# Moving one input load from SyncE's DMA queue to ScalarE's in a fused attention and feed-forward kernel

## The chip, the cores and the metric

The kernel runs on one NeuronCore of a Trainium2 chip. The metric is the device time of one execution in microseconds (us). "Span" is the length of the profiled execution; it is about 2 us shorter than the device time of the same run (323.9 against 325.91 in the profiled run of before).

A "granted clock" is TensorE's clock as a share of full speed. Each run lists its mean over the span. Of the twelve profiles with a windows view by the microsecond, the seven with a mean of 0.997 to 1.0 show 1.00 in every microsecond from 8 to 16 us, and the five with 0.990 to 0.994 show 0.50 there, for 3.4 us in the change, sync_last and v_first and for 6.8 to 6.9 us in cold_before and v_small (summed from the windows). Runs without a profile are sorted below by the same mean (under 0.9965 or not); where their low stretch lay is inferred. The clock record of a trace begins with the first rise of the clock (at 5.11 us in before). Before that the windows view prints 1.00, which is not a measurement: in before the weight loads of the warm-up matmuls come 0.43 us apart until then, and 12 in 2.47 us afterwards.

## The reference, cut to what matters

Linear attention with position weights, then a gated feed-forward layer. Inputs are float32, q, k and v of shape 8 x 8 x 576 x 64 (batch, heads, positions, head size), gate and value weights of 512 x 1536, output weights of 1536 x 512.

```python
r = np.maximum(x, 0.0)                      # for q and for k
phi = concatenate([r * cos_w, r * sin_w])   # cos and sin of the position
kv  = einsum('bhsf,bhsd->bhfd', k_p, v);  z = k_p.sum(axis=2)
x   = (q_p @ kv) / (q_p @ z + 1e-6)
g, val = x @ w_gate, x @ w_val
out = (gelu(g) * val) @ w_out
```

## The kernel before

TensorE is the busy engine for nearly the whole run (98% of the span). Only the first batch has nothing to hide behind: its q, k and v must arrive, be scaled by cosines (VectorE) and sines (ScalarE), and be transposed and multiplied, before TensorE has its long matmuls. The program order on each engine is fixed by hand. The parts that matter:

```python
def load(eng, name, b, m0, m1, j0=0, j1=R):      # R = 9 column groups of 64
    ...
    eng.dma_start(out=staged[name, b][:, m0:m1, j0 * D:j1 * D],
                  in_=rows(srcs[name], b)[:, m0:m1, j0 * D:j1 * D])

load(nc.sync, "k", 0, 0, 2)            # 576 KB, pieces of 2304 B
load(nc.sync, "k", 0, 2, 4)            # 576 KB
load(nc.sync, "q", 0, 0, NP, 0, JA)    # 512 KB, pieces of 1024 B (JA = 4)
load(nc.sync, "v", 0, 0, 2)            # 576 KB, pieces of 2304 B
load(nc.sync, "v", 0, 2, 4)            # 576 KB
load(nc.sync, "q", 0, 0, NP, JA, R)    # 640 KB, pieces of 1280 B
# ... ScalarE: a table load, sin_t, cos_t, a table load, a warm-up Gelu
...
# VectorE and ScalarE, in this order: k's cosines and sines, then
prep("q", 0, 0, range(JA))             # VectorE: q's cosines (L162)
cast_v(0, 0, 2, dve_copy)              # VectorE: v's first half to bf16 (L179)
nc.gpsimd.tensor_copy(gate, staged["v", 0][:, 0, 0:1])  # holds the weight loads back (L458)
load_w(0, 2)                           # GpSimd's queue: gate and value weights
...
dummies(22)                            # TensorE: warm-up matmuls on zeros (L140)
sines(0, 1, 2, 3)                      # ScalarE: q's sines (L160)
turn_j(0, 0, 2, (0, 1), 0, act_copy)   # TensorE: transposes of q (L204), copied out
cast_v(0, 2, 4, dve_copy)              # VectorE: v's second half
turn_j(0, 2, 4, (0, 1), 1, dve_copy)
kv_pairs(0, 0, 2, (6, 7))              # TensorE: k-v products (L218)
turn_j(0, 0, 2, (2, 3), 2, act_copy)
turn_j(0, 2, 4, (2, 3), 3, dve_copy)
...
kv_pairs(0, 2, 4, (4, 5))
...
nm_pair(0, 0, (6, 4))                  # TensorE: q times kv, two tiles (L307)
... # then the first block's gate and value products by tile (L372), and from L400 on the long ones
```

## Time and profile before

| | before |
|---|---|
| median of the first three runs | 326.79 us (326.55 to 327.45) |
| span of the profile | 323.9 us |
| TensorE busy | 98% of the span |
| bytes of the first batch's six loads | 3.54 MB |

The page gives the span, and the busy time and share of TensorE (PE), its weight loads (PEld), VectorE (DVE), ScalarE (ACT) and GpSimd (POOL). Its part on the chain that ended last follows:

```profile
PE 316.8 (98%) x2451; PEld 164.5 (51%) x2451; DVE 170.3 (53%) x407; ACT 159.3 (49%) x336; POOL 26.0 (8%) x43
PE 93%; DMA 2%; DVE 2%; SPq 1%; issue 0%; DVEq 0%
```

The chain of waits in order of time (start, duration, what) shows what the 2% of DMA are: the landing of v's second half, at 10.74 us, and then its cast.

```profile
2.82 7.92 DMA vf<-in_v_dram
10.74 0.02 issue
10.76 0.86 DVE vx L179
```

The DMA issues of the first 14 us give size and time from issue to landing. SyncE issued q's first part at 1.76, so it landed at 1.76 + 6.1 = 7.9.

```profile
vf<-in_v_dram SPq DMA_DIRECT2D x2, 576.0 KB, 7.5
qf<-in_q_dram SPq DMA_DIRECT2D x1, 512.0 KB, 6.1
```

The windows view gives, for each microsecond: its length, busy time (and instructions) of PE, PEld, DVE, ACT, POOL, then the granted clock, the DMA engines' share, and GB/s. The DMA engines are full (a share of 1.06 from 7 to 8 us and 1.46 from 13 to 14).

```profile
7.00:8.00 1.00, 1.00 (x6) 0.35 (x4) 1.00 (x2) 1.00 (x5) 0.90 (x1) 1.00 1.06 417
13.00:14.00 1.00, 0.95 (x20) 0.65 (x17) 0.93 (x5) 1.00 (x4) 0.41 (x1) 1.00 1.46 202
```

The timeline (start, duration, engine, line, operation, output<-input, count, and the idle time before it with what ended it) gives the opening's order:

```profile
1.52 6.67 PE L140 MATMUL ps<-dummy 128*128 128x512 bf16 x22 [1.52 <-POOL dummy L113]
8.09 1.13 DVE L162 TENSOR_SCALAR qp<-qf,cos_t 128x256 bf16<-128x256 f32 x4
8.52 1.69 ACT L160 ACTIVATE qp<-qf,sin_t 128x256 bf16<-128x256 f32 x4
9.06 0.23 PE L204 MATMUL ps<-ident,qp 128*128 128x128 bf16 x1 [0.87 <-ACT qp L160]
9.37 0.77 DVE L179 CAST vx<-vf 128x1152 bf16<-128x1152 f32 x1 [0.15 <-DMA vf<-in_v_dram]
9.39 0.77 POOL L458 COPY gate<-vf 128x1 f32<-128x1 f32 x1 [1.50 <-DMA vf<-in_v_dram]
12.59 0.76 PE L307 MATMUL ps<-kv_sb,qT 128*128 128x65 bf16 x16
16.48 0.61 PE L372 MATMUL ps<-xT,wg_sb 128*128 128x128 bf16 x8
21.11 1.03 PE L400 MATMUL ps<-xT,wg_sb 128*128 128x512 bf16 x4
```

Each input lands just before the engine that needs it is free: q just before 8.09, v's first half 0.15 us late for VectorE.

### The profile page before, as it was taken

To read this page: it belongs to the slowest core of one execution; us is meant where nothing else is said; L and a number is where in the kernel's file an instruction comes from. 1 tells how busy PE (TensorE), PEld (TensorE's weight loads), DVE (VectorE), ACT (ScalarE), POOL (GpSimd) and SP (SyncE) were. 2 spreads that over 40 slices of the span, in tenths; PEclk is the share of its full clock that TensorE was granted. 3 is DMA by queue.
4 is the path that set the end of the run, shared out by engine and by line. 5 is a ranking of instruction groups with operands and counts; after the bars stand their busy time and mean duration, and the time that the engine had idled before them with its cause. 6 is when DMAs were issued, how large, how long until landed. Compare 5 with 4: busy or idle time off the path is not lost.

```text
span 323.9 us, 6340 instructions
## 1 busy us (share of the span) xinstructions
PE 316.8 (98%) x2451; PEld 164.5 (51%) x2451; DVE 170.3 (53%) x407; ACT 159.3 (49%) x336; POOL 26.0 (8%) x43
## 2 busy tenths in 40 slices
PE   8899999999999999999999999999999999999995
PEld 3574556555754564545544554445544444444443
DVE  5854677759665952793586348544532222222211
ACT  7864858946466832673457336633222332222220
POOL 6684410000000000000000000000000000000000
PEclk9999999999999999999999999999999999999999
DMA  7999999842999689938957990543431111111124
GB/s 274 249 186 273 297 352 366 230 111 51 323 216 354 166 147 383 201 83 251 330 96 157 383 232 1 137 102 78 85 73 33 34 32 32 35 32 32 34 65 98
DMA packets 69102, 53.57 MB, mean 165 GB/s; under 512 B 45392, under 2 KB 54352, under 8 KB 69072
## 3 DMA queue, kind: packets, MB, share of 16 engines
q1 hardware_dynamic: 59264, 41.23, 48.1%
q0 software_dynamic: 9648, 11.80, 15.7%
q8 instruction: 19, 0.31, 0.4%
q10 hardware_dynamic: 160, 0.13, 0.1%
q14 instruction: 11, 0.09, 0.1%
HBM read 37.75 MB, written 9.44 MB: 146 GB/s over the span
## 4 chain that ended last, share of the span: by engine, by line
PE 93%; DMA 2%; DVE 2%; SPq 1%; issue 0%; DVEq 0%
PE ps L400 57%; PE ps L430 28%; PE ps L282 3%; PE ps L241 3%; DMA vf<-in_v_dram 2%; PE ps L204 1%; PE ps L372 1%; PE ps L697 1%; SPq L80 1%; PE ps L357 0%; DVE qp L162 0%; DVE x_sb L322 0%; DVE vx L179 0%; DVE x_sb L295 0%; DVE qT L486 0%
## 5 line engine op out<-in xcount | busy, mean ns | idle before, releaser
L409 DVE TENSOR_TENSOR hT<-gel,ps 128x512 bf16<-128x512 f32 (+1 forms) x114 | 74.1, 650 | 128.9 <-PE ps L400 126.0
L408 ACT ACTIVATE gel<-ps 128x512 f32<-128x512 f32 (+1 forms) x114 | 64.8, 569 | 109.7 <-PE ps L400 108.0
L400 PE MATMUL ps<-xT,wv_sb 128*128 128x512 bf16 (+1 forms) x456 | 110.2, 364 | 0.0
L400 PE MATMUL ps<-xT,wg_sb 128*128 128x512 bf16 (+1 forms) x456 | 110.2, 364 | 0.0
L430 PE MATMUL ps<-wo_sb,hT 128*128 128x512 bf16 x420 | 105.8, 379 | 0.0
L400 PEld LDWEIGHTS <-wv_sb 128*128 128x128 bf16 x456 | 44.6, 98 | 47.0
L400 PEld LDWEIGHTS <-wg_sb 128*128 128x128 bf16 x456 | 44.0, 98 | 46.1
L430 PEld LDWEIGHTS <-hT 128*128 128x128 bf16 x420 | 38.3, 98 | 39.4
L439 ACT COPY o_sb<-ps 128x512 f32<-128x512 f32 x34 | 19.9, 587 | 29.9 <-PE ps L430 27.6
L160 ACT ACTIVATE qp<-qf,sin_t 128x256 bf16<-128x256 f32 x72 | 32.0, 501 | 0.4 <-DMA qf<-in_q_dram 0.4
L160 ACT ACTIVATE kp<-kf,sin_t 128x256 bf16<-128x256 f32 (+1 forms) x73 | 29.9, 479 | 0.9 <-DMA kf<-in_k_dram 0.9
L295 DVE TENSOR_TENSOR x_sb<-ps,rec 128x512 bf16<-128x512 f32 x38 | 26.3, 691 | 1.3
L162 DVE TENSOR_SCALAR qp<-qf,cos_t 128x256 bf16<-128x256 f32 x71 | 21.8, 353 | 2.3 <-DMA qf<-in_q_dram 2.3
L282 PEld LDWEIGHTS <-qT 128*128 128x128 bf16 x304 | 14.6, 98 | 7.9 <-ACT qT L486 0.3
L162 DVE TENSOR_SCALAR kp<-kf,cos_t 128x256 bf16<-128x256 f32 x63 | 18.3, 349 | 0.0
L282 PE MATMUL ps<-kv_sb,qT 128*128 128x65 bf16 x304 | 16.0, 194 | 0.0
L179 DVE CAST vx<-vf 128x1152 bf16<-128x1152 f32 (+1 forms) x15 | 12.0, 804 | 0.8 <-DMA vf<-in_v_dram 0.8
L250 ACT CAST kv_sb<-ps 128x260 bf16<-128x260 f32 x14 | 4.6, 383 | 12.9 <-PE ps L241 12.9
L241 PEld LDWEIGHTS <-kp 64*128 64x128 bf16 x504 | 8.5, 95 | 3.0 <-issue 3.0
L140 PE MATMUL ps<-dummy 128*128 128x512 bf16 x27 | 8.4, 457 | 1.5 <-POOL dummy L113 1.5
L241 PE MATMUL ps<-vx,kp 64*128 64x65 bf16 x504 | 9.3, 191 | 0.0
L294 DVE RECIPROCAL rec<-den 128x8 f32<-128x8 f32 x38 | 7.7, 203 | 1.3
(60 smaller groups left out, 100.6 us busy)
## 6 DMA issues: line engine op xcount, KB each, us to landing
out_dram<-o_sb SPq DMA_DIRECT2D x70, 128.0 KB, 2.6
kf<-in_k_dram SPq DMA_DIRECT2D x12, 576.0 KB, 6.2
vf<-in_v_dram SPq DMA_DIRECT2D x12, 576.0 KB, 8.3
qf<-in_q_dram SPq DMA_DIRECT2D x10, 576.0 KB, 5.0
qf<-in_q_dram POOLq DMA_DIRECT2D x4, 576.0 KB, 12.2
kf<-in_k_dram POOLq DMA_DIRECT2D x4, 576.0 KB, 12.5
vf<-in_v_dram POOLq DMA_DIRECT2D x4, 576.0 KB, 12.8
wg_sb<-in_moe_w_gate_dram POOLq DMA_DIRECT2D x6, 256.0 KB, 6.4
```

Of the source, the lines that this page charges most:

```text
L140: nc.tensor.matmul(bank(to), lhsT=dummy[:, 0:128], rhs=dummy, start=True, stop=True)
L160: nc.scalar.activation(o, i, AF.Relu, scale=tab[:, j:j + 1])
L162: (eng or nc.vector).tensor_scalar(o, i, 0.0, tab[:, j:j + 1], op0=ALU.max, op1=ALU.mult)
L179: copy(vx_tiles[b % 2][:, m0:m1, j0:j1, 0:D], staged["v", b][:, m0:m1, j0 * D:j1 * D].rearrange("p m (j d) -> p m j d", d=D),)
L241: nc.tensor.matmul(bank(6 + i)[:, m * (D + 1):(m + 1) * (D + 1)], lhsT=kp[rr, m, j, :], rhs=vx[rr, m, j, :], start=(j == 0), stop=(j == R ...
L282: nc.tensor.matmul(bank(b0 + h // 4)[:, (h % 4) * (D + 1):(h % 4 + 1) * (D + 1)], lhsT=q_cols(b, t, h), rhs=kv_sb[b][:, h // 2, h % 2, :], ...
L295: nc.vector.tensor_tensor(x, nm[:, :, :, 0:D], rec[:, :, :, None].to_broadcast([128, 2, 4, D]), op=ALU.mult,)
L400: nc.tensor.matmul(bank(b0 + g)[:, 0:w], lhsT=wt[:, ct, js], rhs=xt[:, ct, c0:c0 + w], start=(ct == 0), stop=(ct == CT - 1),)
L408: nc.scalar.activation(gel[:, 0:w], bank(b0)[:, 0:w], AF.Gelu)
L409: nc.vector.tensor_mul(hT[n][:, jt, c0:c0 + w], gel[:, 0:w], bank(b0 + 1)[:, 0:w])
L430: nc.tensor.matmul(bank(to), lhsT=hT[n][:, jt, tt * 128:(tt + 1) * 128], rhs=wo_sb[:, jt, :], start=(jt == 0), stop=(jt == JT - 1),)
L439: copy(o_sb, bank(to))
```

## The change

The intent: two queues side by side, so that v need not queue behind q, and SyncE has one issue less.

```diff
     load(nc.sync, "k", 0, 0, 2)
     load(nc.sync, "k", 0, 2, 4)
-    load(nc.sync, "q", 0, 0, NP, 0, JA)
     load(nc.sync, "v", 0, 0, 2)
@@
     nc.scalar.activation(warm, half_pi, AF.Gelu)
+    load(nc.scalar, "q", 0, 0, NP, 0, JA)
```

## The prediction

> **What bounds the kernel now.** The page of the run before gives PE 98% of a 323.9 us span, and the chain of waits is 93% PE. From 19.1 us on TensorE hardly waits, so the change can only act in the opening. There the chain reads: SyncE's five issues (0.7 to 2.8 us), "DMA vf<-in_v_dram" for 7.92 us until v's second half lands at 10.74, VectorE's cast of it, qT copies, kv_sb, q's cosines, den/rec/x_sb, and TensorE from 16.1 us. What delays this chain delays everything after, nearly one for one.
>
> **What the opening waits for.** The windows view shows DMA saturated: share about 1.0 and 330 to 417 GB/s in every microsecond from 3 to 11. The six loads are 3.54 MB, which is what had moved by 12 us. So the order of bytes matters, not the time of issue: an issue costs 0.44 to 0.53 us on SyncE, while 576 KB take about 1.5 us. Landings, from issue and time to landing: k 4.5 and 5.9, q's first part 7.9, v 9.4 and 10.7, q's rest 12.4. Each comes just before its use: ScalarE's k sines end at 8.5 and its q sines run 8.52 to 10.2; VectorE's q cosines start at 8.09.
>
> **What the change does.** It takes one 0.47 us issue off SyncE (v is issued 0.5 us sooner, worth nothing behind a full queue) and puts one of about 0.54 us (ScalarE's two issues at the trace's end) on ScalarE after the warm-up Gelu, which ends at 4.0. ScalarE waits for k until 4.52 anyway. [...] So 512 KB of q will interleave with k or v instead of standing between them.
>
> When it is issued is my largest doubt: between 1 and 4.1 us. Near 4, q shares with v: k is untouched, q's packets (1024 B) alternate with v's (2304 B), and q lands between 8 and 10.7 us. Earlier (ScalarE's sequencer ahead of its table load), q slows k: k's second half lands 1 to 1.7 us later, q at 7.5 to 9.3. In both, v's second half stays near 10.7, since the same bytes precede it, and q's rest near 12.4. VectorE and ScalarE run in order and are nearly full from 4.5 to 12 us, so ScalarE's q sines move by 1 to 2 us, and VectorE's v casts, which stand behind the q cosines, by 0.3 to 1.9 us; its 0.6 us wait before the second cast absorbs part. Net: +0.5 to +1.9 us; I take +1.0. A gain would need v to land clearly sooner, which the bytes forbid.
>
> **Prediction.** 327.8 us, 8 times in 10 between 326.4 and 329.3. Faster by over 2%: 1%; within 2%: 97%; slower by over 2%: 2%.
>
> **What would show it right.** q's first part landing after 7.9 or k's second half after 5.9; v's second half still at 10.5 to 10.9; ScalarE's first q sine after 8.5; the second v cast after 10.76; the first full-width gate matmul (21.1 us) later by as much as the span. After that the timelines should be alike.
>
> **What would make it wrong.** The queues may share by bytes, so that q lands at 8.0 and nothing moves (0 to +0.2 us). ScalarE's queue may get more than its share. TensorE's gap after the warm-up matmuls (8.2 to 9.1 us) may grow to 3 us and cool its clock (about +1 us). v's first half landing sooner would release the weight loads against q's rest. None of these reaches 2% (6.5 us).

The sum: it came to +0.5 to +1.9 us, of which +1.0 was taken, on the 326.8 us of before. The "about +1 us" for a cooled clock stands outside the sum; it was the author's estimate.

## The result, and the profile after

| | before | after |
|---|---|---|
| median of six runs | 326.67 us (325.52 to 327.49) | 329.54 us (329.27 to 329.91) |
| span of the profile | 323.9 us | 327.3 us |
| mean granted clock | 0.998 | 0.992 |

The ratio is 1.0088, with a 95% interval of 1.0066 to 1.0111: slower by some 0.9%, well inside the 2%. A ratio here is the mean time of one kernel's runs over that of the other's of the same rounds, so it is not quite the ratio of the medians. The difference of the medians is 2.87 us.

The chain of waits in order of time now begins with q:

```profile
2.10 8.72 DMA qf<-in_q_dram
```

The DMA issues of the first 14 us: q takes 8.7 us instead of 6.1, and lands at 10.8.

```profile
vf<-in_v_dram SPq DMA_DIRECT2D x2, 576.0 KB, 7.2
qf<-in_q_dram ACTq DMA_DIRECT2D x1, 512.0 KB, 8.7
```

The timeline, the same operations as before:

```profile
1.52 6.53 PE L140 MATMUL ps<-dummy 128*128 128x512 bf16 x22 [1.52 <-POOL dummy L112]
2.10 0.51 ACTq L80 DMA_DIRECT2D qf<-in_q_dram  x1
8.14 0.18 POOL L458 COPY gate<-vf 128x1 f32<-128x1 f32 x1 [0.19 <-DMA vf<-in_v_dram]
10.84 1.70 ACT L160 ACTIVATE qp<-qf,sin_t 128x256 bf16<-128x256 f32 x4 [2.21 <-DMA qf<-in_q_dram]
10.85 1.27 DVE L162 TENSOR_SCALAR qp<-qf,cos_t 128x256 bf16<-128x256 f32 x4 [2.63 <-DMA qf<-in_q_dram]
11.41 0.23 PE L204 MATMUL ps<-ident,qp 128*128 128x128 bf16 x1 [3.36 <-ACT qp L160]
12.03 1.42 DVE L179 CAST vx<-vf 128x1152 bf16<-128x1152 f32 x2
15.86 0.77 PE L307 MATMUL ps<-kv_sb,qT 128*128 128x65 bf16 x16
19.84 0.61 PE L372 MATMUL ps<-xT,wg_sb 128*128 128x128 bf16 x8
24.48 1.03 PE L400 MATMUL ps<-xT,wg_sb 128*128 128x512 bf16 x3
```

Four things are to be seen.

1. The issue is at 2.10, as the first sine activation starts (2.09), long before the warm-up Gelu that stands ahead of it in the program (3.80). The trace shows that the issue waited neither for the second table load (2.51) nor for the Gelu, and not why.
2. v's first half is there by 8.14, but its cast runs at 12.03. VectorE has q's cosines ahead of it in program order, and q is not there.
3. The lag grows. The first transpose is 2.35 us late (11.41 against 9.06), the two-tile products 3.27 us (15.86 against 12.59), the first long matmul 3.37 us (24.48 against 21.11), the span 3.4 us.
4. TensorE now idles 3.36 us ahead of the first transpose.

The growth of the third goes with the fourth: without that gap, in warm_after below, the loss is 1.86 us. In the windows view the clock is at half soon after the first transpose (0.82 in the microsecond from 11 to 12, 0.98 in 15 to 16):

```profile
9.00:10.00 1.00, 0.00 (x0) 0.00 (x0) 0.00 (x0) 0.00 (x0) 1.00 (x3) 1.00 1.07 390
12.00:13.00 1.00, 0.90 (x14) 0.64 (x14) 1.00 (x3) 1.00 (x3) 0.00 (x0) 0.50 1.41 190
13.00:14.00 1.00, 1.00 (x37) 0.91 (x34) 0.78 (x2) 0.02 (x1) 0.54 (x2) 0.50 1.44 194
```

The clock record has one stretch of 3.412 us at 0.5 there, from 11.64 to 15.05. It begins 0.23 us after the gap of 3.36 us ends. In other profiles single gaps of 3.04 us (v_small), 3.14 (sync_last) and 3.91 (cold_before) between the warm-up and the first transposes came with a half clock too, and the longest waits before the first transposes of 0.87 (before), 1.37 (warm31), 1.69 (before18) and 1.96 us (early_issue) did not. Length alone does not sort them: in v_first, below, gaps of 1.18 and 1.93 us with 0.75 us of matmuls between them came with a half clock. What decides within this range is not shown.

Why q came so late is in the DMA queues' own packets (count, MB, share of the engines' time), q1 being SyncE's queue and q10 ScalarE's. From 4 to 5 us, and from 7 to 8 us:

```profile
q1 hardware_dynamic: 179, 0.41, 104.0%
...
q1 hardware_dynamic: 124, 0.26, 67.7%
q10 hardware_dynamic: 122, 0.12, 36.2%
```

Up to 5 us ScalarE's queue moved nothing, though q was issued at 2.10. Its first packet in the trace's DMA records starts at 5.61, after k's 512 packets (the 512th packet of 2304 B starts at 5.26). From 7 us on the two queues move packets in nearly equal number: 124 against 122, then 118 against 118 and 165 against 162 in the next two microseconds. A packet of q is 1024 B and one of v is 2304 B, so q gets a third of the bytes (0.12 of 0.39 MB from 7 to 8 us) and its 512 packets last nearly as long as v's 512: v's last packet starts at 9.8 and q's at 10.4, where before q's started at 7.53. The starts in the DMA records go with the counts: from 4 to 5 us the distances between packets of q1 pile up at 89 ns and its multiples, and from 7 to 8.6 us those within either queue pile up at 132 ns and its multiples. A packet of q1 takes 93 ns there and one of q10 46 (medians). I read this as one packet of each in turn; the records do not name the engine of a packet, so the turns themselves are not seen.

### The profile page after: what moved, and what is told of

Its sections match the earlier page's. It is cut to its first block, busy times and chain, and to the rows that moved or that the text cites. A ratio compares the mean times of both kernels' runs of the same rounds, so it can differ in the third digit from the quotient of the medians. Undisturbed runs are those within 1.5% of the kernel's fastest.

```text
span 327.3 us, 6303 instructions
## 1 busy us (share of the span) xinstructions
PE 315.3 (96%) x2414; PEld 165.3 (51%) x2451; DVE 170.6 (52%) x407; ACT 159.3 (49%) x336; POOL 25.3 (8%) x43
## 4 chain that ended last, share of the span: by engine, by line
PE 93%; DMA 3%; DVE 1%; issue 1%; ACT 0%; POOL 0%; DVEq 0%; POOLq 0%
PE ps L400 56%; PE ps L430 27%; PE ps L282 3%; PE ps L241 3%; DMA qf<-in_q_dram 3%; PE ps L204 1%; PE ps L372 1%; PE ps L697 1%; PE ps L357 1%; PE ps L218 1%; DVE qp L162 0%; ACT qp L160 0%; DVE x_sb L295 0%; DVE vx L179 0%; PE ps L140 0%
## 5 line engine op out<-in xcount | busy, mean ns | idle before, releaser
L430 PE MATMUL ps<-wo_sb,hT 128*128 128x512 bf16 x401 | 103.1, 379 | 1.4 <-issue 0.8
L204 PE MATMUL ps<-ident,qp 128*128 128x128 bf16 x72 | 6.8, 239 | 3.8 <-ACT qp L160 3.5
```

The source lines that it names most:

```text
L204: nc.tensor.transpose(out=dst[:, n * 128:(n + 1) * 128], in_=phi["q", b][:, m, j, :], identity=ident,)
L430: nc.tensor.matmul(bank(to), lhsT=hT[n][:, jt, tt * 128:(tt + 1) * 128], rhs=wo_sb[:, jt, :], start=(jt == 0), stop=(jt == JT - 1),)
```

## The experiments

My theory after the result: the queue does not matter, the order in which the bytes land does. q's last byte now comes behind most of v. This costs some 2 us by itself, and the idle gap it makes costs about 1 us more through the clock. The rivals: ScalarE's issue or its queue is slow; the clock is harmless; what costs is that the programs wait for q ahead of v. The medians of before on the same chip were 326.82 us for the first four experiments, 327.18 for the next two, 326.75 for the four after them and 326.85 for the last two.

| run | median, us | ratio to before (95% interval) | runs with a mean clock under 0.9965 |
|---|---|---|---|
| the change | 329.54 | 1.0088 (1.0066 to 1.0111) | 6 of 6 |
| sync_last | 329.41 | 1.0075 (1.0051 to 1.0099) | 3 of 4 |
| warm_after | 328.56 | 1.0057 (1.0040 to 1.0074) | 0 of 4 |
| cold_before | 327.48 | 1.0016 (0.9991 to 1.0041) | 4 of 4 |
| v_first | 329.49 | 1.0081 (1.0056 to 1.0105) | 4 of 4 |
| early_issue | 327.06 | 1.0021 (0.9989 to 1.0053) | 1 of 4 |
| v_small | 329.92 | 1.0072 (1.0023 to 1.0120) | 3 of 4 |
| warm31 | 329.06 | 1.0084 (1.0061 to 1.0108) | 2 of 6 |
| v_first_warm | 328.25 | 1.0046 (1.0029 to 1.0062) | 1 of 6 |
| before_again | 327.17 | none (one run) | 0 of 1 |
| before18 | 326.34 | 0.9993 (0.9975 to 1.0011) | 0 of 6 |
| gate_on_q | 326.77 | 1.0005 (0.9979 to 1.0032) | 3 of 6 |
| gate_on_q18 | 326.24 | 0.9991 (0.9968 to 1.0015) | 1 of 6 |

All gave correct results.

### The order alone, without ScalarE's queue (sync_last)

```diff
-    load(nc.sync, "q", 0, 0, NP, 0, JA)
     load(nc.sync, "v", 0, 0, 2)
     load(nc.sync, "v", 0, 2, 4)
+    load(nc.sync, "q", 0, 0, NP, 0, JA)
     load(nc.sync, "q", 0, 0, NP, JA, R)
```

> All six loads stay on SyncE, in the order k, k, v, v, q's first part, q's rest: ScalarE issues nothing. Theory (what costs is that q's last byte now arrives behind v's; the queue that carries it does not matter): q's first part lands near 10.6 us, v near 8.0 and 9.3, the first transposes start near 11.3, the clock drops as in the changed kernel, and the time is that of the changed kernel, before + 2.5 to 3.5 us. Rival (ScalarE's own issue, or a slow start of its queue, costs the time): time of before, within 0.7 us.

The timeline of this kernel, then its windows (columns as before):

```profile
10.47 1.71 ACT L160 ACTIVATE qp<-qf,sin_t 128x256 bf16<-128x256 f32 x4 [2.05 <-DMA qf<-in_q_dram]
```

```profile
13.00:14.00 1.00, 1.00 (x35) 0.91 (x30) 0.62 (x2) 0.00 (x0) 0.12 (x2) 0.50 1.40 189
```

With everything on SyncE and only q's place moved behind v, q's work starts at 10.47, the clock drops, and the time is, within the intervals, that of the change (1.0075 against 1.0088). ScalarE's queue is cleared: the change is, in effect, a reordering of the loads.

### The clock alone (warm_after, warm31, cold_before)

```diff
-    dummies(22)
+    dummies(37)      # warm_after, on the changed kernel
+    dummies(31)      # warm31, on the changed kernel
+    dummies(8)       # cold_before, on the kernel before
```

> The changed kernel with 37 warm-up matmuls instead of 22, so that TensorE is busy until q is there. Theory (about 2.4 us of the loss is q's lateness, about 0.9 us is TensorE's clock at 0.5 between 11.8 and 15 us): no drop of the clock, first transposes still near 11.4, the two-tile attention products near 15.0 instead of 15.86, time before + 1.8 to 2.6 us, about 0.9 below the changed kernel. Rival (the clock is harmless because the vector engines bound the opening): time unchanged against the changed kernel, before + 2.7 to 3.4 us.

> The kernel before with 8 warm-up matmuls instead of 22: TensorE idles from about 4.9 to 9.1 us, all loads as they were. Theory: the idle gap alone drops the clock to 0.5 for about 3 us from the first transposes on and costs 0.6 to 1.1 us. Rival (the clock is harmless): within 0.3 us of before.

> The changed kernel with 31 warm-up matmuls. With 37 they overshot: in that profile the clock rose only at 7.4 us, they ended at 12.5 and held up transposes whose q was ready at 11.7. With 31 they should end between 9.8 and 11.4 wherever the clock rises. Theory (the clock costs about 1 us of the loss, the rest is q's lateness): no drop of the clock in any run, time before + 1.5 to 2.2 us. Rival (the clock's part is all of it, and q's lateness is hidden): before + 0 to 0.7 us.

In warm_after no run had a low stretch, and the loss fell from 2.87 to 1.86 us (0.57% of 326.7). The windows and the timeline show how: TensorE is busy while it waits (1.00 in every microsecond from 8 to 12), the clock stays at 1.00, and the two-tile products come at 15.40 instead of 15.86.

```profile
9.00:10.00 1.00, 1.00 (x7) 0.44 (x5) 0.00 (x0) 0.00 (x0) 1.00 (x3) 1.00 1.05 389
13.00:14.00 1.00, 0.75 (x37) 0.70 (x38) 1.00 (x3) 0.33 (x1) 0.00 (x0) 1.00 1.43 191
```

```profile
15.40 0.77 PE L307 MATMUL ps<-kv_sb,qT 128*128 128x65 bf16 x16
```

Useless matmuls made the kernel faster by 0.9 us (its four runs took 328.44 to 328.93, the change's six 329.27 to 329.91; the means are 328.62 and 329.54). The two did not run in the same rounds, and the intervals of their ratios overlap. I thought 37 overshot (the first transposes came at 12.33, not near 11.4), and tried 31. This was a miss as a tuning: two of its six runs still met a low stretch. But it gives a difference within one kernel: its four warm runs have a mean of 328.83, its two others of 330.44, 1.6 us more. early_issue below has the same split (three runs with a mean of 327.03, one of 328.63); in sync_last it is 1.2 us and in v_first_warm 0.7. So a low stretch goes with about 0.7 to 1.6 us here. That the clock alone makes this difference within a kernel is not shown: in the runs that were not profiled q may also have landed later.

cold_before was to measure that on the kernel before. It lost 0.16%, about 0.5 us, and its interval (0.9991 to 1.0041) includes no loss at all as well as the 0.6 to 1.1 us that I expected. That is inconclusive. Its windows show the clock at 0.5 from about 8.8 to 15.7 us, twice as long as in the change, and its opening did lag: the two-tile products came at 14.12, against 12.59 and 12.94 in the two profiles of before.

```profile
14.12 1.08 PE L307 MATMUL ps<-kv_sb,qT 128*128 128x65 bf16 x16
```

Before's own scatter, told of below, may hide a part of this; no run tested it. Whether the low clock costs the same there as in the changed kernel stays open.

### The programs follow the new order (v_first, v_first_warm)

```diff
-    prep("q", 0, 0, range(JA))
     cast_v(0, 0, 2, dve_copy)
+    cast_v(0, 2, 4, dve_copy)
+    prep("q", 0, 0, range(JA))
@@
     dummies(22)
+    kv_pairs(0, 0, 2, (6, 7))
+    dummies(6, 0)                   # v_first_warm only
     sines(0, 1, 2, 3)
     turn_j(0, 0, 2, (0, 1), 0, act_copy)
-    cast_v(0, 2, 4, dve_copy)
     turn_j(0, 2, 4, (0, 1), 1, dve_copy)
-    kv_pairs(0, 0, 2, (6, 7))
```

> The changed kernel with its loads, but VectorE's two casts of v ahead of the q cosines, and the first k-v products ahead of the q transposes on TensorE: the programs follow the new order of arrival. Theory (part of the loss is that work on v, which is there at 8.1 and 10.2, stands in program order behind work on q, which comes at 10.8): casts at 8.2 and 10.3, first k-v products near 9.0, shorter idle gap, time before + 0.8 to 1.8 us. Rival (q's arrival alone sets the end of the opening): time of the changed kernel, before + 2.5 to 3.4 us.

> The kernel with v's work ahead of q's, and six filling matmuls between the first k-v products and the transposes, since the profile without them showed the clock at 0.5 from 12.3 us on. Theory (order of the programs matters once the clock no longer hides it): no drop of the clock, time before + 0.6 to 1.6 us, and 0.5 us or more below the changed kernel with 31 warm-up matmuls. Rival (q's arrival alone sets the end of the opening): the same as that kernel within 0.3 us.

v_first moved v's work ahead of q's as intended, yet took the time of the change: 1.0081. By its expectations the rival had won. But its windows showed the clock at 0.5 from 13 to 15 us and at 0.51 in the next, so the clock hid the answer:

```profile
13.00:14.00 1.00, 1.00 (x12) 1.00 (x11) 0.67 (x2) 0.59 (x2) 0.01 (x1) 0.50 1.42 184
```

With six filling matmuls the loss is 0.46%, 1.5 us (one of its six runs still had a mean clock of 0.993, where I expected none). The timeline of v_first_warm:

```profile
9.79 0.75 PE L218 MATMUL ps<-vx,kp 64*128 64x65 bf16 x36 [1.62 <-POOL gate L459]
14.88 0.77 PE L307 MATMUL ps<-kv_sb,qT 128*128 128x65 bf16 x16
```

The products of q come at 14.88, and the mean of its five warm runs is 328.12, 0.5 us below warm_after and 0.7 below warm31's warm runs. The profiles bear this out (14.88 against 15.40, and 15.37 in warm31), though the intervals of the ratios overlap. So the order of the programs seems worth about half a microsecond; the 1.5 us that are left I put down to q's lateness itself.

### When ScalarE issues, and the size of the packets (early_issue, v_small)

```diff
# early_issue, on the changed kernel: q's load moves here, ahead of ScalarE's
# first table load (its line after the warm-up Gelu goes)
+    load(nc.scalar, "q", 0, 0, NP, 0, JA)
     load(nc.sync, "k", 0, 0, 2)
# v_small, on the changed kernel: v in packets of 1024 and 1280 B
-    load(nc.sync, "v", 0, 0, 2)
-    load(nc.sync, "v", 0, 2, 4)
+    for m in (0, 2):
+        load(nc.sync, "v", 0, m, m + 2, 0, JA)
+        load(nc.sync, "v", 0, m, m + 2, JA, R)
```

> The changed kernel with q's load put ahead of ScalarE's table load, so that it is issued near 0.75 us with k's first half instead of at 2.10. Theory (an issue's packets stand behind those of earlier issues until these are drained, then the two queues alternate packet by packet): q's 512 packets alternate one for one with k's 512, q lands near 7.3, k's halves near 5.1 and 7.3 instead of 4.5 and 5.9, v's at about 9.4 and 10.7; time before + 0.5 to 1.6 us. Rival (ScalarE's queue needs some 3.5 us to start whatever is in front of it): q's first packet near 4.2 us, k lands as before, time near before.

> The changed kernel with each half of v loaded in two pieces, of 4 and of 5 columns of 64, so that v's packets are 1024 and 1280 B (q's are 1024) instead of 2304 B. Theory (the queues alternate packet by packet, so the larger packets take the larger share of bytes): q gets nearly half the bytes and lands at 8.4 to 9.3 us instead of 10.8, v's second half still near 10.7; time before + 0.2 to 1.5 us. Rival (the share does not depend on the packet's size: bytes, or a fixed preference for SyncE): q lands at 10.5 to 10.9, time of the changed kernel.

In early_issue, q was issued at 0.74 and landed at 6.0; k's first half was used from 5.07 and its second from 7.49, 1.6 us later than before. From 3 to 4 us:

```profile
q1 hardware_dynamic: 94, 0.22, 56.9%
q10 hardware_dynamic: 96, 0.10, 33.6%
```

Again nearly one for one. So ScalarE's queue has no fixed start of 3.5 us: here 19 of its packets had moved by 3.0 us, 2.3 us after the issue. The time is within noise of before (1.0021), but the interval (0.9989 to 1.0053) holds the 0.5 to 1.6 us that I expected too, so a cost of that size is neither shown nor excluded. Late k moves ScalarE's q sines to 10.13, but VectorE's second v cast still ends at 11.7, as before (11.6); the last short product with the value weights starts at 22.0, and so the first long matmul at about that time, between those of before's two profiles (21.11 and 22.34).

In v_small from 7 to 8 us:

```profile
q1 hardware_dynamic: 166, 0.20, 57.7%
q10 hardware_dynamic: 166, 0.17, 51.1%
```

With packets of nearly one size, equal numbers of packets come to nearly the same bytes (0.20 and 0.17 MB). In the change the packets came in nearly equal number too (124 against 122), and the bytes did not (0.26 against 0.12 MB): in these two profiles it is the packets that were shared evenly. The landing was a miss: q came at 10.2, not at 8.4 to 9.3, as a last 30 of its 512 packets went between 9 and 10 us. The time was one of two, of which only the first lies within the 0.2 to 1.5 us that I expected: 327.39 in the one run without a low stretch, 329.88 to 329.99 in the others, whose mean clock was 0.990 (its profile has a stretch of about 6.9 us at half clock).

### Why before itself scatters (before_again, before18, gate_on_q, gate_on_q18)

Before's own spans lie between 323.8 and 325.5; in the fourteen runs of the first two sets of experiments they seemed to form two groups. As its first profile was one of the fastest, differences between two profiles (3.4 us of span) overstate the difference of the medians (2.87 us).

```diff
-    dummies(22)
+    dummies(18)                                             # before18, gate_on_q18
-    nc.gpsimd.tensor_copy(gate, staged["v", 0][:, 0, 0:1])
+    nc.gpsimd.tensor_copy(gate, staged["q", 0][:, 0, 0:1])  # gate_on_q, gate_on_q18
```

> The kernel before, for a second profile, because its own runs fall into two groups of span (323.8 to 324.2 and 324.6 to 325.4 us). Theory: the groups differ by when the clock first rises during the warm-up matmuls (4.9 us in the first profile): a profile with a longer span shows a rise at 6 us or later and warm-up matmuls that end after 9.0. Rival: the loads land at other times.

> The kernel before with 18 warm-up matmuls instead of 22. If the longer spans of before come from warm-up matmuls that overrun q's arrival, 18 of them end by 9.0 us even when the clock rises late: 0.2 to 0.6 us faster than before on average, unless the longer idle gap when the clock rises early drops it again in some runs, which would show as runs of a lower mean clock and a time over 1 us longer.

> The kernel before, with the weight loads released by the landing of q's first part (7.9 us) instead of v's first half (9.4 to 9.7). Theory (before's longer spans come from the first value-weight load, which landed at 18.1 in the second profile while TensorE wanted it at 17.3; the changed kernel never waits for it, because v's earlier landing released the weights 1.8 us sooner): no wait for the weights, all runs at or below the faster runs of before, on average 0.3 to 0.8 us below before. Rival (weights sooner compete with v and q's rest for the DMA engines and delay v): the same or slower than before.

> The same with 18 warm-up matmuls instead of 22. Theory: the count does not matter in the kernel before, as the warm-up ended at 8.2 and 8.4 us in both its profiles, ahead of the transposes at 9.06: within 0.3 us of the kernel with 22. Rival (22 overrun in some runs): 0.2 to 0.5 us faster than that.

My theory of the warm-up count was wrong. The second profile of before (span 325.2) had its warm-up over at 8.36. It waited elsewhere, for the first value weights:

```profile
18.15 0.62 PE L372 MATMUL ps<-xT,wv_sb 128*128 128x128 bf16 x8 [0.81 <-DMA wv_sb<-in_moe_w_val_dram]
22.34 1.03 PE L400 MATMUL ps<-xT,wg_sb 128*128 128x512 bf16 x3
```

The weight loads are held back until v's first half lands. In the changed kernel that is at 8.1 instead of 9.4 to 9.7, so its weights come early, and TensorE never waits for them in its profile. I read that as a small gain within the change. Measured against this second profile, the change's first long matmul is 2.1 us late (24.48 against 22.34), as is its span (327.3 against 325.2).

Releasing the weights by q's landing removed the wait from gate_on_q's profile, and its three runs without a low stretch have spans of 323.7 to 324.1. But three others had a mean clock of 0.994 to 0.995 and took 1.6 us more, so the mean is that of before. Neither these kernels nor before18 is clearly faster than before: no version here beats it beyond its scatter. Before itself has a few runs at 0.995 as well. Where in all those runs the low stretch lay was not profiled.

## Why the prediction was wrong

The direction, the place and the verdict within 2% held. The size did not: I said 327.8, at most 329.3, and it was 329.54, a loss of 2.87 us where I had +1.0.

- Held: "the order of bytes matters, not the time of issue". sync_last shows it without ScalarE's queue. But the time of issue sets that order: issued at 0.74, q landed at 6.0 (early_issue), issued at 2.10 at 10.8.
- Held: only the opening could change. The lag was 3.37 us at the first long matmul and 3.4 us at the end.
- Held as a mechanism, just missed as a number: "q's packets (1024 B) alternate with v's (2304 B), and q lands between 8 and 10.7 us". The packets came in equal number (118 of each queue from 8 to 9 us), and q landed at 10.8. That it came so near was partly luck: this branch was meant for an issue near 4 us. The issue was at 2.10, and its packets started only at 5.6, which I had not foreseen.
- Failed, a mis-sized term: "Net: +0.5 to +1.9 us; I take +1.0". I took a middle of two branches. The branch that came true was at its end: q landed at 10.8, and without the clock the loss is 1.86 us (warm_after).
- Failed, a term left out of the sum: the gap that "may grow to 3 us and cool its clock (about +1 us)" stood among the things that would make the prediction wrong. It was not a separate risk. The q at 10.8 made the gap 3.36 us, with 3.4 us at half clock after it, so the two had to be added: my own 1.9 and 1 make 2.9, against 2.87 us measured. warm_after splits the measured loss into 1.86 us and 0.9 to 1.0, so the size of this term was about right.
- Failed: "Earlier (ScalarE's sequencer ahead of its table load), q slows k". The issue was early, at 2.10, and k was used at 4.58 and 5.90 as before. q's packets did not start until k's had (5.61 against 5.26 for the last of k's). With an issue at 0.74 (early_issue) k did lose 1.6 us; what that cost the whole is lost in the noise. So "early" and "late" did not divide where I put the border: an issue at 2.10 was already late.
- Failed: "v's second half still at 10.5 to 10.9". It was issued at about 2.24 and took at most 8.0 us, so it landed near 10.2 in that profile. But that gained nothing, as VectorE was waiting for q. (In v_first's profile, with the same loads, VectorE waited for it until 10.92, so this figure scatters.)

What stays open: why the packets of a later issue start late. Issued at 2.10, q's started at 5.61, after k's 512; issued at 0.74, q's went one for one with SyncE's (96 against 94 from 3 to 4 us), then ahead of them (247 against 68 from 4 to 5 us). The traces show this and not its rule.

## What to carry to other kernels

Here the DMA engines were already full, and the second queue added no bandwidth (417 GB/s before and 385 after, from 7 to 8 us). It changed which load landed last, and the load with packets of 1024 B lost against the one with 2304 B (0.12 against 0.26 MB in that microsecond). So ask of such a change which consumer now waits, in what order the engines' programs expect their inputs, and whether the wait leaves TensorE idle for long enough to lose its clock (here gaps of 3.04 to 3.91 us came with a half clock, and so did 1.18 and 1.93 close together, but not a single 1.96); where the last is so, add its cost to the wait's, as the two came together (about 0.9 us on top of 1.86). Read the mean clock of each run before comparing times below 1%.
